# TensorE's order in the last chunk of an attention and expert kernel: the early tokens' transposes moved, the first products spread over the last routing

## The chip, the core and the metric

The kernel runs on one core of a Trainium2 chip. A core has five engines with queues of their own: TensorE (PE), which multiplies matrices, VectorE (DVE), ScalarE (ACT), GpSimd (POOL) and SyncE (SP), which issues most transfers. Each engine executes its queue in order. Engines wait for each other by semaphores. The metric is the device time of one execution in microseconds; the time before is the median of three runs, 338.18 us (337.67 to 339.53).

## The reference

Two stages. The first is a linear attention with decay, over 4 batches, 8 heads, 768 steps and 48 dimensions a head:

```
for t in range(S):
    cur = einsum('bhd,bhe->bhde', u * kt, vt)
    y[:, :, t] = einsum('bhd,bhde->bhe', rt, state + cur)
    state = wt[..., None] * state + einsum('bhd,bhe->bhde', kt, vt)
```

The second takes the 3072 rows of y (384 wide). A row with `x @ w_skip > 0` goes to the expert, of eight, with the largest `x @ w_gate`; its output is `x + gate * (relu(x @ w1[e]) @ w2[e])`, with the softmax's value as gate and w1 of 384x1024, w2 of 1024x384. Other rows are copied.

## The kernel before

**Chunks.** The sequence is cut into 24 chunks of 128 steps (6 per batch). A loop over s from -2 to 24 (L545) runs a software pipeline with everything in the order in which it is written: in turn s the keys of chunk s+2 are scaled (`prep_*`, DVE), the scores of chunk s+1 are made (`intra`, L292, PE) and masked (`mask`, L298, DVE), the bonus of the current step is made (`bonus_sums`, L307, PE; `bonus`, L311, DVE, which writes it to PSUM as the start of y), and y of chunk s is summed on top of it (`outputs`: L342 from the scores, L347 from the state). `evict` (L352, ACT) copies y, `rows_out` (L357, PE) turns it into rows with the logits beside them, and `store` (L365, L367, ACT; L368, SP) takes logits and rows out one turn later.

**Routing.** Chunks are routed in four groups of six. `router` is a generator: `drip` runs it on by one piece at a time, from places between the steps above, and `flush` emits what it left for PE or ACT in the list `held`. It makes the one-hot of each row's expert (`oh`, L398), each row's rank within its expert by small products on PE (`ranks`, L401 to L406, to the bank `pss`), one-hots of the ranks (`hot`, L436), the gates in three parts (`vals`, L423, L446, L449), and with them tables of row numbers and gates by expert and rank (`places`, L459 and L462).

**The early expert.** After three groups (`LATE` = 18 chunks) expert 0 has 128 tokens already. `early` gathers their rows (L488, POOL, to `xg0`); `early_tokens(0)` transposes them (L502, PE, in a PSUM buffer of the two that bear the tag `psT`, which `rows_out` and the keys' transposes share) and copies them to `xT0` (L503, ACT). `early_expert` is a generator too, of 24 first-layer products of 128x128 (L112 by `hidden`, in two groups of 12, each evicted twice by ACT, L521 and L523, and once by DVE, L510), and 24 second-layer products (L532). Each yields a price, 214 or 160.

**The last routing.** After the loop, from L623, the last group's router runs alone. Each turn there drips it, flushes, adds `STEP` to the account `due` and emits early products until their prices have used it up. Then come the indices (`idr`, L633, DVE), the gather of expert 0's second 128 tokens (L615, POOL, `xg1`), the early products that remain but for the last four, the transposes of the second tokens (`early_tokens(1)`, L502), and the four.

**Experts.** The experts follow in order (`expert`), with expert 0's second tokens first (L112 again, then L733 to L735); each uses weights in a high and a low part (split on ACT and DVE, L86 and L87), and its rows are gathered by POOL (L615) and scattered back (L677).

Of the kernel before, what the change touches and what calls it, by code (L numbers as in the profile page):

```python
# [32 lines left out]
Q_MAX = 1e12  # L33
LATE = 18
NHB = 11
STEP = 230
W_AT = 4
Q_MIN = 1e-30
RW = 1 + NP * CW + 3 * NP * P + 3
# [14 lines left out]
def rwkv_moe_kernel(ctx, tc, wrk, wrk0, vN, uP, wgs, wgp, w12, cst, out):  # L54
# [7 lines left out]
    n = len(seq)  # L62
# [47 lines left out]
    def hidden(ps, xT, fc, kc):  # L110
        o = kc * DF + fc * P
        return nc.tensor.matmul(ps, raws[0, 0][:, o:o + P], xT[:, kc], start=(kc == 0),  # L112
                                stop=(kc == KC - 1))
# [5 lines left out]
    with tc.tile_pool(name="att", bufs=2) as att, \  # L119
# [105 lines left out]
        def drip(k=1):  # L225
            for _ in range(k):
                while later and next(later[0], None) is None:
                    later.popleft()

        work, lgs, gens = {}, {}, {}  # L230
        pace = [1]
# [38 lines left out]
        def prep_check(i):  # L270
            wk = work[i]
            w3 = wk["w"][:, 1:1 + NP * CW].rearrange("p (a j) -> p a j", a=NP)[:, :, :P]
            junk = att.tile([P, NP, P], BF16, tag="junk", name=f"junk{i}", bufs=1)
            nc.scalar.activation(junk, w3, AF.Relu, bias=bias_lo, scale=-1.0,
                                 accum_out=viol[:, i:i + 1])
            nc.scalar.copy(q0all[:, i], wk["q"][:, :, 0])
# [200 lines left out]
        def early():  # L477

            ps = ps1.tile([P, 512], F32, tag="psT", name="psC", bufs=2)[0:1, 0:1]
            nc.tensor.matmul(ps, onesb[:, 0:1], ohs[:, 0, 0:1], start=True, stop=True)  # L480
            short = att.tile([1, 1], F32, tag="short", name="short", bufs=1)
            nc.vector.tensor_scalar(short, ps, -1.0, float(P), op0=ALU.mult, op1=ALU.add)
            yield 1
            nc.vector.scalar_tensor_tensor(ohs[0:1, 0, 0:1], short, 0.0, ohs[0:1, 0, 0:1],
                                           op0=ALU.max, op1=ALU.add)
            yield 1
            nc.vector.tensor_tensor(id0, tab[:, 0, 0, 0:1], tab[:, 0, 1, 0:1], op=ALU.add)
            nc.gpsimd.indirect_dma_start(  # L488
                out=xg[0], out_offset=None, in_=out[:LATE * P],
                in_offset=bass.IndirectOffsetOnAxis(ap=id0, axis=0),  # L490
                bounds_check=LATE * P - 1, oob_is_err=False)
            yield 1
            nc.vector.tensor_reduce(gate0, tab[:, 0, 2:NV, 0], axis=AX, op=ALU.add)
            for _ in range(6):
                yield 1
            early_tokens(0)
            yield 1

        def early_tokens(j):
            ps = ps1.tile([P, KC, P], F32, tag="psT", name=f"psX0{j}", bufs=2)  # L500
            for kc in range(KC):
                nc.tensor.transpose(ps[:, kc], xg[j][:, kc * P:(kc + 1) * P], ident)  # L502
            nc.scalar.copy(xT0[j], ps)  # L503
# [9 lines left out]
        def early_expert():  # L513
            for g in range(2):
                ps = ps1.tile([P, NP, P], F32, tag=f"psA{g}", name=f"psH0_{g}")
                for f in range(NP):
                    for kc in range(KC):
                        hidden(ps[:, f], xT0[0], NP * g + f, kc)
                        yield 214
                fs = slice(NP * g, NP * (g + 1))  # L520
                nc.scalar.activation(h0h[:, fs], ps, AF.Relu)  # L521
                hf = att.tile([P, NP, P], F32, tag="asb", name=f"hf{g}", bufs=4)
                nc.scalar.activation(hf, ps, AF.Relu)  # L523
                hfs.append((h0l[:, fs], hf, h0h[:, fs].bitcast(F32)))
            pso = ps1.tile([P, DM], F32, tag="psB", name="psO0")
            w2h, w2l = wsp[0, 2], wsp[0, 3]
            todo = [(h0h, fc, w) for fc in range(FC) for w in (w2h, w2l)]
            todo += [(h0l, fc, w2h) for fc in range(FC)]
            for i, (h, fc, w) in enumerate(todo):
                if i == len(todo) - FC:  # L530
                    early_low(FC)
                nc.tensor.matmul(pso, h[:, fc], w[:, fc * DM:(fc + 1) * DM],  # L532
                                 start=(i == 0), stop=(i == len(todo) - 1))
                yield 160
            nc.vector.scalar_tensor_tensor(fin0, pso, gate0, xg[0], op0=ALU.mult, op1=ALU.add)
# [6 lines left out]
        with tc.manual_schedule():  # L542
            setup()
            fill(FILL0)
            for s in range(-2, n + 1):  # L545
                on = lambda i: 0 <= i < n
                if s + 4 < n:
                    load_chunk(s + 4)
                if on(s + 3) and s + 3 >= 1:
                    load_v(s + 3)  # L550
                if s == -2:
                    nc.sync.dma_start(c_sb[:, C_IOTA:], cst[:, C_IOTA:])
                    nc.sync.dma_start(wgp_sb, wgp)
                if s == -1:
                    nc.sync.dma_start(wgs_sb, wgs)
                if on(s - 1):
                    store(s - 1)
                for i0, m in GROUPS:
                    if i0 + m == s:
                        pace[0] = 1 if i0 + m < LATE else 2  # L560
                        later.append(router(i0, m))
                        if i0 + m == LATE:
                            later.append(early())
                if on(s):
                    update(s)
                    carry(s)
                if on(s + 2):
                    prep_scan(s + 2)
                drip(pace[0])
                if on(s):  # L570
                    outputs(s)
                flush()
                if on(s + 2):
                    prep_keys(s + 2)
                    drip(pace[0])
                    prep_reads(s + 2)
                if on(s):
                    evict(s)
                if on(s + 1):
                    intra(s + 1)  # L580
                    drip(2 * pace[0])
                    mask(s + 1, 0)
                    mask(s + 1, 1)
                    drip(pace[0])
                    bonus_sums(s + 1)
                    bonus(s + 1)
                if on(s + 2):
                    prep_check(s + 2)
                if on(s):
                    rows_out(s)  # L590
                flush()
                if s == -2:
                    nc.vector.tensor_copy(trib, tri)
                    nc.gpsimd.tensor_copy(identb, ident)
                    nc.gpsimd.tensor_copy(iota, c_sb[:, C_IOTA:C_IOTA + 2 * P])
                k = s + 1 - W_AT
                for eq, k0 in (((0, 1), 0), ((0, 0), 3), ((1, 0), 8), ((1, 1), 16)):
                    if k == k0:
                        gens[eq] = load_weights(*eq)
                    if k0 <= k < k0 + 3:  # L600
                        next(gens[eq])
                if 1 <= k < 7:
                    split_slice(0, 5 + k, nc.gpsimd)
                if 9 <= k < 15:
                    split_slice(1, k - 9, nc.gpsimd)
# [15 lines left out]
        ids = keep.tile([P, 2, E], U32, name="ids")  # L621
        gates = keep.tile([P, 2, E], F32, name="gates")
        with tc.manual_schedule(engines={nc.tensor.engine, nc.scalar.engine, nc.vector.engine}):  # L623
            todo, due, done = early_expert(), 0, [0]
            while later:
                drip(pace[0])
                flush()
                due += STEP
                while due > 0:
                    due -= next(todo, 1 << 20)  # L630
                    done[0] += 1
            with nc.allow_low_precision(reason="whole numbers"):
                nc.vector.tensor_reduce(idr, pt[:, :, 0:2].rearrange("p j q e -> p j e q"),  # L633
                                        axis=AX, op=ALU.add)
            gather(1, None)
            early_low(1)
            nc.vector.tensor_reduce(gates, pt[:, :, 2:].rearrange("p j q e -> p j e q"),
                                    axis=AX, op=ALU.add)
            nc.vector.tensor_scalar(idf, gates, 0.0, BIG, op0=ALU.is_equal, op1=ALU.mult)
            nc.vector.tensor_tensor(ids, idf, idr, op=ALU.add)  # L640
            for k in range(done[0], 6 * FC - 4):
                next(todo)
            early_tokens(1)
            drain(todo)
# [269 lines left out]
```

## Time and profile before

| | |
|---|---|
| median of three runs | 338.18 us (337.67 to 339.53) |
| the profiled execution, its time | 338.03 us |
| its span, first to last instruction | 336.2 us |
| mean granted clock of PE | 0.951 of full speed |
| PE busy | 300.8 us (89%) |
| DVE, ACT, POOL busy | 253.4, 174.6, 85.9 us |
| read and written in HBM | 52.76 and 7.86 MB |

The span starts at 0; times in the rows below are microseconds from there, durations in nanoseconds are called so. A row of the timeline gives the start, the length, the engine and line, the operation, what it writes and reads, and how many instructions are merged in it; a bracket tells how long the engine stood idle ahead of it and what ended that. A product in full precision is two instructions of PE in the profile (x6 is three products). The granted clock is the share of full speed at which PE's clock ran in a stretch. In the span, chunks end near 180 us, the last routing near 187, and experts fill the rest.

### The profile page before, as it was taken

To read this page: it belongs to the slowest core of one execution; us is meant where nothing else is said; L and a number is where in the kernel's file an instruction comes from. 1 tells how busy PE (TensorE), PEld (TensorE's weight loads), DVE (VectorE), ACT (ScalarE), POOL (GpSimd) and SP (SyncE) were. 2 spreads that over 40 slices of the span, in tenths; PEclk is the share of its full clock that TensorE was granted. 3 is DMA by queue.
4 is the path that set the end of the run, shared out by engine and by line. 5 is a ranking of instruction groups with operands and counts; after the bars stand their busy time and mean duration, and the time that the engine had idled before them with its cause. 6 is when DMAs were issued, how large, how long until landed. Compare 5 with 4: busy or idle time off the path is not lost.

```text
span 336.2 us, 7539 instructions
## 1 busy us (share of the span) xinstructions
PE 300.8 (89%) x2845; PEld 279.7 (83%) x2845; DVE 253.4 (75%) x472; ACT 174.6 (52%) x479; POOL 85.9 (26%) x88
## 2 busy tenths in 40 slices
PE   7499998898979989599696999999999999999990
PEld 2388887897869878488585999999999999999990
DVE  5899999899998999999524357859494949585410
ACT  4357666586384864556612255838282828273300
POOL 7312124433233334211200177240202020111111
PEclk9789999799997999979969899999999999999996
DMA  8999999999999887783301149984736373630000
GB/s 234 247 228 216 252 249 263 242 244 210 187 283 254 179 186 162 149 221 111 110 2 47 25 128 329 391 289 144 259 112 261 106 257 126 256 153 23 7 27 12
DMA packets 23104, 60.40 MB, mean 180 GB/s; under 512 B 4103, under 2 KB 10667, under 8 KB 23057
## 3 DMA queue, kind: packets, MB, share of 16 engines
q1 hardware_dynamic: 20576, 53.69, 59.4%
q0 software_dynamic: 2048, 5.48, 4.9%
q10 hardware_dynamic: 432, 0.66, 0.6%
q8 instruction: 24, 0.39, 0.5%
q14 instruction: 24, 0.19, 0.2%
HBM read 52.76 MB, written 7.86 MB: 180 GB/s over the span
## 4 chain that ended last, share of the span: by engine, by line
PE 59%; DMA 19%; DVE 9%; issue 5%; POOL 4%; SPq 2%; ACT 0%; POOLq 0%; DVEq 0%
DMA vt<-wrk 10%; DMA wrk<-wrk 7%; PE psO L735 6%; PE psO L733 6%; PE psO L734 6%; PE psH L715 6%; PE psH L714 6%; PE psH L713 6%; PE psY L342 4%; PE psY L347 3%; PE psA L292 3%; PE psB L307 3%; PE psH L112 3%; POOL rk L262 2%; DVE asb L298 2%
## 5 line engine op out<-in xcount | busy, mean ns | idle before, releaser
L262 POOL TENSOR_TENSOR rk<-wrk 128x512 f32<-128x512 f32 x24 | 30.7, 1279 | 105.8 <-PE psA L292 31.8
L720 ACT ACTIVATE hh<-psH 128x256 fp32r<-128x256 f32 x60 | 23.0, 383 | 55.8 <-PE psH L715 52.5
L715 PE MATMUL psH<-xTh,w1l 128*128 128x256 f32 x168 | 47.5, 283 | 0.0
L714 PE MATMUL psH<-xTl,w1h 128*128 128x256 f32 x168 | 47.5, 283 | 0.0
L713 PE MATMUL psH<-xTh,w1h 128*128 128x256 f32 x168 | 47.5, 283 | 0.0
L677 POOL DMA_INDIRECT out<-fin,ids x16 | 16.8, 1049 | 101.6 <-DVE fin L740 94.7
L342 PE MATMUL psY<-asb,v 128*48 128x128 f32 x384 | 28.2, 294 | 14.2 <-DVE psY L311 14.1
L733 PE MATMUL psO<-w2h,hh 128*128 128x384 f32 x120 | 40.7, 339 | 0.0
L298 DVE TENSOR_TENSOR asb<-psA,c_sb 128x512 f32<-128x512 f32 x48 | 30.8, 683 | 12.8 <-PE psA L292 12.8
L735 PE MATMUL psO<-w2h,hl 128*128 128x384 f32 x120 | 40.1, 334 | 0.0
L734 PE MATMUL psO<-w2l,hh 128*128 128x384 f32 x120 | 40.1, 334 | 0.0
L242 DVE TENSOR_TENSOR_SCAN q<-wrk,smask 128x516 f32<-128x516 f32 x24 | 34.4, 1435 | 3.7 <-DMA wrk<-wrk 3.7
L342 PEld LDWEIGHTS psY<-asb,v 128*48 128x48 f32 x384 | 21.9, 132 | 16.2 <-DVE psY L311 15.7
L721 DVE SCALAR_TENSOR_TENSOR hl<-psH,hh 128x256 fp32r<-128x256 f32 x60 | 25.2, 420 | 12.2 <-ACT hh L720 11.8
L715 PEld LDWEIGHTS psH<-xTh,w1l 128*128 128x128 f32 x168 | 32.2, 192 | 0.0
L714 PEld LDWEIGHTS psH<-xTl,w1h 128*128 128x128 f32 x168 | 32.2, 192 | 0.0
L713 PEld LDWEIGHTS psH<-xTh,w1h 128*128 128x128 f32 x168 | 32.2, 191 | 0.0
L292 PE MATMUL psA<-rp,kq 64*128 64x128 f32 x384 | 29.6, 296 | 1.2 <-DVE rp L259 1.2
L740 DVE SCALAR_TENSOR_TENSOR fin<-psO,gates,xg 128x384 f32<-128x384 f32 x15 | 9.3, 618 | 28.3 <-PE psO L735 28.3
L292 PEld LDWEIGHTS psA<-rp,kq 64*128 64x128 f32 x384 | 25.0, 199 | 5.7 <-issue 3.9
L255 DVE TENSOR_TENSOR_SCAN rh<-wrk,dstart 128x516 f32<-128x516 f32 x24 | 29.3, 1223 | 0.0
L87 DVE TENSOR_TENSOR w2l<-r,w2h 128x512 fp32r<-128x512 f32 x42 | 27.8, 687 | 1.1 <-ACT w2h L86 0.2
(137 smaller groups left out, 658.3 us busy)
## 6 DMA issues: line engine op xcount, KB each, us to landing
r<-w SPq DMA_DIRECT2D x48, 512.0 KB, 5.6
wrk<-wrk SPq DMA_DIRECT2D x46, 288.9 KB, 5.9
v<-vN SPq DMA_DIRECT2D x24, 192.0 KB, 5.6
out<-x SPq DMA_DIRECT2D x24, 192.0 KB, 5.0
vt<-wrk SPq DMA_DIRECT2D x46, 96.0 KB, 5.7
wrk<-wrk SPq DMA_DIRECT2D x1, 258.5 KB, 3.9
wrk<-wrk ACTq DMA_DIRECT2D x1, 256.0 KB, 4.1
wrk<-wrk SPq DMA_DIRECT2D x1, 256.0 KB, 4.6
```

Of the source, the lines that this page charges most:

```text
L242: nc.vector.tensor_tensor_scan(q.rearrange("p a j -> p (a j)")[:, ::-1], t[:, 1:1 + n_][:, ::-1], smask_f[:, ::-1], 0.0, op0=ALU.mult, op1 ...
L255: nc.vector.tensor_tensor_scan(rh.rearrange("p a j -> p (a j)"), wk["w"][:, 0:NP * CW], dstart.rearrange("p a j -> p (a j)"), 0.0, op0=ALU ...
L262: mul = nc.gpsimd.tensor_tensor(rk.rearrange("p a j -> p (a j)"), wk["w"][:, R_OFF:K_OFF], wk["w"][:, K_OFF:V_OFF], op=ALU.mult)
L292: nc.tensor.matmul(wk["psa"][g][:, a], wk["kq"][rows, a], wk["rp"][rows, a], start=True, stop=True)
L298: nc.vector.tensor_tensor(s, wk["psa"][g], tri.rearrange("p (o j) -> p o j", o=1).to_broadcast([P, NP, P]), op=ALU.mult)
L342: nc.tensor.matmul(psy[64 * g:64 * g + D, a], v[:, 2 * a + g], wk["asb"][g][:, a], start=False, stop=(c == 0), skip_group_check=True)
L713: nc.tensor.matmul(ps, w1h[:, o:o + P], xTh[:, kc], start=(kc == 0), stop=False)
L714: nc.tensor.matmul(ps, w1h[:, o:o + P], xTl[:, kc], start=False, stop=False)
L715: nc.tensor.matmul(ps, w1l[:, o:o + P], xTh[:, kc], start=False, stop=(kc == KC - 1))
L733: nc.tensor.matmul(pso, h[j, fc][0], w2h[:, o], start=(fc == 0), stop=False)
L734: nc.tensor.matmul(pso, h[j, fc][0], w2l[:, o], start=False, stop=False)
L735: nc.tensor.matmul(pso, h[j, fc][1], w2h[:, o], start=False, stop=(fc == FC - 1))
```

## The change

Two edits in TensorE's order. `early_tokens(0)` was called by `early`, six pieces after its gather, and is now called in the turn of the last chunk, between `evict` and `rows_out`. And the account of the last routing starts at `HEAD * STEP` = 1284 instead of 0, gets 214 a turn instead of 230, and each turn drips the router by one piece instead of two (`pace` is 2 there).

```diff
-STEP = 230
+HEAD = 6
+STEP = 214
@@ early()
             nc.vector.tensor_reduce(gate0, tab[:, 0, 2:NV, 0], axis=AX, op=ALU.add)
-            for _ in range(6):
-                yield 1
-            early_tokens(0)
             yield 1
@@ the loop over s
                 if on(s + 2):
                     prep_check(s + 2)
+                if s == n - 1:
+                    early_tokens(0)
                 if on(s):
                     rows_out(s)
@@ the last routing
-            todo, due, done = early_expert(), 0, [0]
+            todo, due, done = early_expert(), HEAD * STEP, [0]
             while later:
-                drip(pace[0])
+                drip()
                 flush()
                 due += STEP
                 while due > 0:
                     due -= next(todo, 1 << 20)
                     done[0] += 1
```

Lines behind L36 have numbers one higher in the changed kernel, up to L493, and two lower from there to L586 (L502 becomes L500, L112 L113, L342 L343, L532 L530).

PE's queue from the state update of chunk 22 (psu) to the first scores of chunk 23 (psA_23), before. The psX at L502 is the early tokens' transpose, xg_65 their gathered rows:

```order
L320 MATMUL psu<-v_1959,kt_2223 48x48 x8
L502 MATMUL psX_2277<-c_sb,xg_65 128x128 x3
L342 MATMUL psY<-asb_22_2240,v_1959 48x128
L342 MATMUL psY<-asb_22_2242,v_1959 48x128 x2
L342 MATMUL psY<-asb_22_2240,v_1959 48x128 x2
L342 MATMUL psY<-asb_22_2242,v_1959 48x128 x2
L342 MATMUL psY<-asb_22_2240,v_1959 48x128
L347 MATMUL psY<-rp_2110,sblk_110 128x128 x4
```

Now y of chunk 22 follows the update directly; the three transposes are gone from here.

The same queue from the rows of chunk 22 (the first psX) to the start of the last ranks (trib), before, and then of the change. psH is the bank of the early first-layer products, xT_67 the early tokens' transpose:

```order
L357 MATMUL psX_2316<-wgp_sb,xT_2294 128x105 x4
L112 MATMUL psH_0_2366<-xT_67,r_00_816 128x128 x3
L342 MATMUL psY<-asb_23_2306,v_2063 48x128
L342 MATMUL psY<-asb_23_2308,v_2063 48x128 x2
L342 MATMUL psY<-asb_23_2306,v_2063 48x128 x2
L342 MATMUL psY<-asb_23_2308,v_2063 48x128 x2
L342 MATMUL psY<-asb_23_2306,v_2063 48x128
L347 MATMUL psY<-rp_2212,sblk_111 128x128 x4
L357 MATMUL psX_2340<-wgp_sb,xT_2338 128x105 x4
L401 LDWEIGHTS trib
```

```order
L358 MATMUL psX_2311<-wgp_sb,xT_2289 128x105 x4
L343 MATMUL psY<-asb_23_2301,v_2063 48x128
L343 MATMUL psY<-asb_23_2303,v_2063 48x128 x2
L343 MATMUL psY<-asb_23_2301,v_2063 48x128 x2
L343 MATMUL psY<-asb_23_2303,v_2063 48x128 x2
L343 MATMUL psY<-asb_23_2301,v_2063 48x128
L348 MATMUL psY<-rp_2212,sblk_111 128x128 x4
L500 MATMUL psX_2335<-c_sb,xg_65 128x128 x3
L358 MATMUL psX_2340<-wgp_sb,xT_2333 128x105 x4
L113 MATMUL psH_0_2364<-xT_67,r_00_816 128x128 x10
L402 LDWEIGHTS trib
```

The transposes stand between y and the rows of chunk 23; three early products have left the place ahead of its y, and ten stand between its rows and the ranks, where none stood.

From the last product of the ranks to the first of the places, before, and then of the change:

```order
L406 MATMUL pss<-oh_2373,onesb 128x8
L112 MATMUL psH_0_2366<-xT_67,r_00_816 128x128 x7
L459 LDWEIGHTS identb
L459 MATMUL pss<-tab,identb 128x40
L462 LDWEIGHTS hot_0_2396
```

```order
L407 MATMUL pss<-oh_2380,onesb 128x8
L113 MATMUL psH_0_2364<-xT_67,r_00_816 128x128 x2
L113 MATMUL psH_1_2397<-xT_67,r_00_816 128x128 x12
L460 LDWEIGHTS identb
L460 MATMUL pss<-tab,identb 128x40
```

Fourteen early products instead of seven stand here, and all 24 are now ahead of the places; the 14 that followed the places before are gone from there, so that the second-layer products (L532) follow directly. On ACT the evictions of the first group of twelve (L521 and L523) now precede the last routing's gate casts (L422, L423, L446), and on DVE their low part (L510) stands between the indices (L633) and the gates (L637). The queues of POOL and SP are the same.

## The prediction

> **What bounds the kernel now.** I read three views in this order: the engines' busy time by stretch, the rows in order of time around the places where TensorE (PE) has nothing to do, and busy time again on the grid on which the granted clock moves. The first asks whether a gap on PE can be made good later.
>
> ```profile
> span 336.2 us, 7539 instructions
> 200.00:250.00 50.00, 50.00 (x368) 50.00 (x367) 37.67 (x72) 30.00 (x67) 15.32 (x15) 1.00 0.70 248
> ```
>
> From 200 to 250 us (columns: length, busy time of PE, weight loads, DVE, ACT and POOL, then granted clock, DMA share, GB/s) PE works all the time at full clock. What follows the last routing is one queue on PE, so whatever brings the expert products forward brings the end forward. The question is when PE reaches them, and where it stands before. Columns of the next rows: start, length, engine, line, operation; in brackets the idle time ahead and what ended it.
>
> ```profile
> 158.33 1.04 PE L342 MATMUL psY<-asb,v 128*48 128x128 f32 x16
> 159.31 1.16 PE L347 MATMUL psY<-rp,sblk 128*128 128x128 f32 x8
> 161.07 1.16 PE L292 MATMUL psA<-rp,kq 64*128 64x128 f32 x16
> 164.13 0.69 DVE L311 TENSOR_TENSOR psY<-psB,vt 128x512 f32<-128x512 f32 x1
> 164.46 1.23 POOL L488 DMA_INDIRECT xg<-out,id  x1 [0.17 <-issue]
> 168.04 0.87 PE L502 MATMUL psX<-c_sb,xg 128*128 128x128 f32 x3 [3.34 <-DMA xg<-out,id]
> 168.84 1.95 PE L342 MATMUL psY<-asb,v 128*48 128x128 f32 x16
> 170.72 2.08 PE L347 MATMUL psY<-rp,sblk 128*128 128x128 f32 x8
> 172.72 1.57 PE L292 MATMUL psA<-rp,kq 64*128 64x128 f32 x16
> 175.53 0.69 DVE L311 TENSOR_TENSOR psY<-psB,vt 128x512 f32<-128x512 f32 x1
> 176.09 0.85 PE L112 MATMUL psH<-xT,r 128*128 128x128 f32 x6
> 176.88 1.08 PE L342 MATMUL psY<-asb,v 128*48 128x128 f32 x16
> 179.72 1.14 PE L357 MATMUL psX<-wgp_sb,xT 128*128 128x105 f32 x8 [0.68 <-ACT xT L352]
> ```
>
> The transposes of the early tokens (L502) stand ahead of chunk 22's y products (L342), and PE waits 3.34 us for the gather that feeds them. The y products needed only the bonus of DVE (L311), done at 164.13 + 0.69 = 164.82. After the gap they run slowly: 168.84 to 172.80 for y and state reads, where chunk 21 took 158.33 to 160.47. The clock says why. On a grid of 3.41 us, each stretch shows one clock:
>
> ```profile
> 57.59:61.00 3.41, 1.37 (x25) 1.06 (x20) 3.41 (x7) 2.84 (x10) 2.50 (x2) 1.00 1.07 291
> 61.00:64.41 3.41, 3.41 (x20) 3.08 (x21) 3.12 (x7) 1.35 (x3) 0.03 (x1) 0.50 1.03 203
> 78.07:81.48 3.41, 1.88 (x32) 1.66 (x32) 3.41 (x5) 2.19 (x8) 2.32 (x2) 1.00 1.03 201
> 81.48:84.89 3.41, 3.41 (x43) 2.98 (x40) 3.38 (x7) 1.59 (x6) 0.00 (x0) 1.00 1.03 227
> 163.40:166.81 3.41, 1.29 (x24) 1.06 (x22) 1.42 (x4) 2.23 (x8) 2.12 (x2) 1.00 0.27 78
> 166.81:170.23 3.42, 2.19 (x17) 1.88 (x19) 0.00 (x0) 0.48 (x1) 0.00 (x0) 0.50 0.10 37
> 180.47:183.88 3.41, 1.24 (x17) 1.08 (x16) 2.46 (x12) 1.12 (x5) 0.00 (x0) 1.00 0.16 58
> 183.88:187.29 3.41, 3.23 (x28) 3.08 (x27) 2.62 (x14) 0.21 (x1) 0.02 (x1) 0.50 0.00 0
> ```
>
> After a stretch with 1.24 to 1.37 us of PE work the clock is halved, after one with 1.88 it is not. Two gaps of this kernel cost that: the one at 164.7, and the routing's, in these rows:
>
> ```profile
> 182.77 0.21 DVE L398 TENSOR_TENSOR oh<-key,km 128x48 bf16<-128x48 f32 x1
> 183.03 0.18 PE L401 MATMUL pss<-oh,trib 128*128 128x48 bf16 x1 [2.17 <-DVE oh L398]
> 183.21 2.75 PE L112 MATMUL psH<-xT,r 128*128 128x128 f32 x14
> 185.71 0.41 DVE L452 TENSOR_TENSOR sg<-oh,vals 128x240 bf16<-128x240 bf16 x1
> 186.17 0.36 PE L462 MATMUL pss<-sg,hot 128*128 128x40 bf16 x6 [0.18 <-DVE sg L452]
> 186.60 3.69 PE L112 MATMUL psH<-xT,r 128*128 128x128 f32 x28
> 186.80 0.19 DVE L633 TENSOR_REDUCE idr<-pss 128x16 uint32<-128x32 f32 x1 [0.69 <-PE pss L462]
> 187.27 1.00 POOL L615 DMA_INDIRECT xg<-out,idr  x1 [21.59 <-DVE gates L637]
> 193.65 0.49 PE L502 MATMUL psX<-c_sb,xg 128*128 128x128 f32 x3
> 195.05 5.52 PE L112 MATMUL psH<-xT,r 128*128 128x128 f32 x48
> ```
>
> PE waits 2.17 us for the one-hot of experts (L398), works at half clock, and goes without a gap from 186.60 into the products of the second early token tile, at 195.05. That last start is the mark that I carry through the change.
>
> **The change, first part: transposes moved behind y of chunk 23.** No instruction is added or removed; on DVE, ACT and POOL nothing else moves in this part but the copy after the transposes, and no queue of SP or POOL is passed. Chunk 22's y starts at about 164.88 instead of 168.84. At full clock its y and state reads take 2.14 us as for chunk 21 (160.47 − 158.33), so they end at 167.0; its masks, keys, v and state were ready by then, because their row for the bonus, the last of them, is. The scores of chunk 23 take 1.16 as in the row at 161.07, to 168.2. From the end of the scores to the end of the bonus before: 172.72 + 1.57 = 174.29 to 175.53 + 0.69 = 176.22, that is 1.93 of DVE work. So the bonus ends at 170.1 and y of chunk 23 starts at 170.15. Three early products filled PE before this start (0.85 at 176.09); they are gone from here, and PE now rests some 0.2 us at most. From y to the logits' rows it took 179.72 − 176.88 = 2.84, of which 0.68 was a wait for ACT's copy of y. The transposes cost 0.49 (row at 193.65, full clock) and fit in that wait: they are free, and would cost 0.49 if ACT's copy were earlier. Their tokens land at 168.0, some 4 us before they are needed at 172.3. The rows of chunk 23 start at 173.0 instead of 179.72: **6.7 us earlier**. From the other side: 4.0 (start of y) + 1.8 (half clock in y and reads) + 0.4 (scores) + 0.6 (three products) = 6.8.
>
> **Second part: the 24 first products.** One costs 5.52/24 = 0.23 us at full clock; the row of 14 instructions at half clock (7 products in 2.75) bounds it at 0.39. Counting from the rows' start, with 179.72 set to 173.0:
> - ten products now follow the rows: 1.1 + 2.3 = 3.4 after the start. The ranks ran at 3.31 before. Their wait of 2.17 is filled, at a cost of 0.1.
> - 14 instead of seven products stand between ranks and places: 0.2 + 3.2 more, so PE is free for the places at 6.8. The place values (sg) were ready at 186.12, 6.4 after the start. ACT has 1.2 us of evictions more ahead of the gate's casts:
>
> ```profile
> 187.64 0.60 ACT L521 ACTIVATE h0h<-psH 128x512 fp32r<-128x512 f32 x1 [2.17 <-PE psH L112]
> 188.13 0.59 ACT L523 ACTIVATE hf<-psH 128x512 f32<-128x512 f32 x1
> ```
>
>  Their group of twelve products ends some 0.5 after the ranks, so they end near 5.2 after the start. DVE's six one-hots take until then anyway: I take 0.2 for the casts, and the places wait for PE, not for sg. Without that cover the casts would cost up to 1.2.
> - places, 0.43 as before (186.60 − 186.17), then the indices 0.2 later (186.80 − 186.60): PE goes on at 180.3, the indices start at 180.5 and the gather of the second tile at 180.5 + 0.47 = 180.97.
>
> **What is late next.** The 14 products that ran while that gather was under way are gone from behind the places. PE now has only 20 products of the second layer there. Their length is in the chain of waits, and the gather's, from issue to landing, is the last number in the rows of DMA issues; the row of three numbers is for all 15 gathers of line 615:
>
> ```profile
> 190.28 3.53 PE psO L532 x20
> ```
>
> ```profile
> xg<-out,id POOLq DMA_INDIRECT x1, 3.4
> xg<-out,idr POOLq DMA_INDIRECT x1, 4.0
> DMA to landing us min/median/max: 3.0/6.5/8.2
> ```
>
> So PE would come to the transposes at 180.3 + 3.5 = 183.8. The same gather took 4.0, so I take that: landing at 185.0, and PE waits **1.2 us, new**. Behind it in PE's queue stand four second-layer products and all experts. With 3.0, the fastest, the wait is 0.2. From these transposes to the next tile's products it was 195.05 − 193.65 = 1.40, so those start at 186.4.
>
> **Sum.** 195.05 − 186.4 = 8.65 us earlier: 6.7 from the first part, some 3.1 from a routing that no longer waits and runs at full clock, less 1.2 for the new wait. I set it against the profiled execution, 338.03 us (span 336.2 and 1.8 around it): 338.03 − 8.65 = 329.4. The median of the runs shown, 338.18, lies 0.15 above, within what runs differ.
>
> One rule bears on the new wait. In the Trainium skill, "TensorE: Matmul & The Clock Gate", Part 1, the clock halves after an idle window of some 3.4 us; by that alone the 2.17 us at 183.03 would not have halved it, and the wait of 1.2 never could. The trace agrees on the 3.41 but not on the idleness: 1.24 us of work did not save that stretch. Part 4 of that page says that transposes do not count as busy in the same way; no run here shows it.
>
> **Rivals.**
> - *The new wait halves the clock.* If PE's transposes did not count, a stretch of 3.41 with the wait of 1.2 and 0.5 of transposes would have 1.7 us of work, between 1.37 (halved) and 1.88 (not). The price is the next 3.41 us at half speed: 1.7 us, 331.1. Against it: with the transposes it has 2.2, and a stretch that the wait straddles has more. The page's Part 4 is what speaks for it.
> - *The second tile's gather is later.* The row at 187.27 names the gates (L637) as releaser, and 0.69 of DVE work (the low part of the first group) now stands ahead of them: 0.9 more if true; and the slowest landing of such a gather was 8.2, 4.2 more. That gives 330.3 to 333.6. Against it: the gather reads indices, not gates, and nothing else moves on DMA then.
> - *The gain is given back behind 195 us*, by a transfer that doesn't come forward with PE: 336.5 to 338. Against it: the gathers of the other experts and the next weights are released by PE's and DVE's own progress, and PE shows 50.00 of 50.00 there.
> - *Slower than before.* The rows of chunk 23, and with them the whole routing, now stand behind the first gather. If it lands after 172.3, every microsecond costs one; the kernel is slower from a landing at 172.3 + 8.6 = 180.9, which is 16.4 after its issue at 164.46. It took 3.4; the slowest of its kind took 8.2. At a landing of 182 the time would be 339.
> - *The change does not do what it says*: excluded by the order of the instructions, which shows each move.
>
> **How the numbers follow.** My forecast, 328.4 (gather in 3.0) to 330.4, has 0.71. The halved clock has 0.12, the late gather 0.08, the gain given back 0.06, slower 0.02; 0.01 is left below. The range runs from 328.4 to 331.5, which holds the first two and the cheaper half of the third. A measurement of this kernel tells about 0.5%, 1.7 us, from no change. Faster by more than that needs less than 336.5: 0.94; within it 0.04; slower 0.02.
>
> **What would show it.** Right: no PE gap near 165 to 168 and a full clock through both former half-clock stretches; the rows of chunk 23 at 173.0; the transposes between y and rows with no wait; ranks and places without a PE wait above 0.2; a wait of 0.2 to 1.2 at the second tile's transposes; its products at 186.4; and from there the same lengths as before. Wrong: a half clock after 184, a gather of the second tile that lands more than 4 us after its issue, or a new gap among the experts.

## The result, and the profile after

| | before | after |
|---|---|---|
| median of four runs | 338.07 us (337.67 to 339.53) | 328.90 us (328.49 to 329.58) |
| ratio, with its 95% interval | | 0.9723 (0.9697 to 0.9750) |
| the profiled execution: time, span | 338.03, 336.2 us | 328.79, 327.0 us |
| mean granted clock of PE | 0.951 | 0.970 |
| PE busy | 300.8 us (89%) | 296.9 us (91%) |

The kernel is 9.2 us faster; the forecast was 329.4. Below are the same places in the timeline of the changed kernel (start, length, engine, line, operation, and in brackets the idle time ahead and what ended it). Its chunk stage ran 0.43 us later, ahead of anything that was changed: the first row, chunk 22's state update, starts at 164.56, and at 164.13 before (over all traces here at 162.97 to 166.65). So starts are compared from that update on.

```profile
164.56 0.56 PE L321 MATMUL psu<-v,kt 128*48 128x48 f32 x16
165.31 1.08 PE L343 MATMUL psY<-asb,v 128*48 128x128 f32 x16 [0.18 <-DVE psY L312]
166.32 1.16 PE L348 MATMUL psY<-rp,sblk 128*128 128x128 f32 x8
167.41 1.16 PE L293 MATMUL psA<-rp,kq 64*128 64x128 f32 x16
170.55 1.08 PE L343 MATMUL psY<-asb,v 128*48 128x128 f32 x16
172.55 0.49 PE L500 MATMUL psX<-c_sb,xg 128*128 128x128 f32 x3
173.39 1.14 PE L358 MATMUL psX<-wgp_sb,xT 128*128 128x105 f32 x8 [0.35 <-ACT xT L353]
174.37 2.42 PE L113 MATMUL psH<-xT,r 128*128 128x128 f32 x20
176.70 0.18 PE L402 MATMUL pss<-oh,trib 128*128 128x48 bf16 x1
176.88 3.37 PE L113 MATMUL psH<-xT,r 128*128 128x128 f32 x28
179.57 0.41 DVE L453 TENSOR_TENSOR sg<-oh,vals 128x240 bf16<-128x240 bf16 x1
180.08 0.18 PE L460 MATMUL pss<-tab,identb 128*128 128x40 bf16 x1
180.63 0.19 DVE L633 TENSOR_REDUCE idr<-pss 128x16 uint32<-128x32 f32 x1 [0.65 <-PE pss L463]
181.10 1.20 POOL L615 DMA_INDIRECT xg<-out,idr  x1 [14.98 <-DVE idr L633]
184.65 0.52 PE L500 MATMUL psX<-c_sb,xg 128*128 128x128 f32 x3 [0.45 <-DMA xg<-out,idr]
185.98 5.62 PE L113 MATMUL psH<-xT,r 128*128 128x128 f32 x48
```

Read it from above. The wait of 3.34 for the first gather is gone: y (L343) follows the update at once, and y and reads take 1.08 and 1.16 where they took 1.95 and 2.08. The transposes (L500) stand before the rows (L358), and PE then waits 0.35 for ACT's copy where it waited 0.68. The ranks (L402) have no wait. The places (L460) start at 180.08, 0.10 after DVE's place values are ready (179.57 + 0.41 = 179.98): PE and DVE arrive together. The one new wait is the 0.45 at 184.65. The same stretches on the clock's grid (length, then busy time of PE, weight loads, DVE, ACT, POOL, then granted clock, DMA share, GB/s):

```profile
164.93:168.35 3.42, 3.24 (x50) 2.81 (x44) 0.32 (x1) 2.56 (x8) 1.19 (x1) 1.00 0.38 118
175.17:178.59 3.42, 3.42 (x37) 3.33 (x36) 3.11 (x18) 1.23 (x4) 0.00 (x0) 1.00 0.16 58
182.00:185.41 3.41, 2.96 (x19) 2.67 (x18) 0.56 (x1) 0.20 (x1) 1.99 (x3) 1.00 0.28 75
200.00:250.00 50.00, 50.00 (x357) 50.00 (x356) 36.76 (x69) 28.19 (x62) 9.58 (x10) 1.00 0.67 240
```

None of the first three, which hold the former gap at the gather, the ranks and the new wait, has less than 2.96 us of work, and the clock is 1.00 in all. Among the experts PE is busy 50.00 of 50.00, as before: nothing is given back there. From the second tile's products to the end of the span it takes 327.0 − 185.98 = 141.0, before 336.2 − 195.05 = 141.2. From the update to those products it takes 21.42, before 30.92: **9.50 less**. With the 0.43 lost ahead and the 0.13 won behind (unrounded) that is the span's 9.2.

### The profile page after: what moved, and what is told of

It reads as the page before. It is cut to its first block, busy times and chain, and to the rows that moved or that the text cites. A ratio compares the mean times of both kernels' runs of the same rounds, so it can differ in the third digit from the quotient of the medians.

```text
span 327.0 us, 7539 instructions
## 1 busy us (share of the span) xinstructions
PE 296.9 (91%) x2845; PEld 276.2 (84%) x2845; DVE 253.4 (77%) x472; ACT 174.5 (53%) x479; POOL 87.9 (27%) x88
## 4 chain that ended last, share of the span: by engine, by line
PE 64%; DMA 16%; DVE 10%; issue 5%; POOL 2%; SPq 1%; ACTq 0%; POOLq 0%; ACT 0%; DVEq 0%
DMA vt<-wrk 9%; PE psO L734 6%; PE psO L733 6%; PE psO L735 6%; PE psH L715 6%; PE psH L714 6%; PE psH L713 6%; DMA wrk<-wrk 5%; PE psY L343 5%; PE psY L348 4%; PE psA L293 4%; PE psH L113 3%; PE psB L308 3%; DVE asb L299 3%; DVE psY L312 2%
## 5 line engine op out<-in xcount | busy, mean ns | idle before, releaser
L263 POOL TENSOR_TENSOR rk<-wrk 128x512 f32<-128x512 f32 x24 | 31.6, 1318 | 104.7 <-PE psA L293 34.7
L343 PE MATMUL psY<-asb,v 128*48 128x128 f32 x384 | 27.3, 288 | 14.8 <-DVE psY L312 14.7
L243 DVE TENSOR_TENSOR_SCAN q<-wrk,smask 128x516 f32<-128x516 f32 x24 | 33.5, 1395 | 4.1 <-POOL wrk L198 2.2
L343 PEld LDWEIGHTS psY<-asb,v 128*48 128x48 f32 x384 | 21.3, 129 | 16.7 <-DVE psY L312 16.6
```

What stands on the lines that cost most here:

```text
L243: nc.vector.tensor_tensor_scan(q.rearrange("p a j -> p (a j)")[:, ::-1], t[:, 1:1 + n_][:, ::-1], smask_f[:, ::-1], 0.0, op0=ALU.mult, op1 ...
L263: mul = nc.gpsimd.tensor_tensor(rk.rearrange("p a j -> p (a j)"), wk["w"][:, R_OFF:K_OFF], wk["w"][:, K_OFF:V_OFF], op=ALU.mult)
L343: nc.tensor.matmul(psy[64 * g:64 * g + D, a], v[:, 2 * a + g], wk["asb"][g][:, a], start=False, stop=(c == 0), skip_group_check=True)
```

## The experiments

Theory T is the prediction's: the end follows one queue on PE; the first part brings the rows forward by removing a blocked transpose and a halved clock, the second fills the routing's waits. Unless a text on record says otherwise, every kernel below computes the whole reference. "Landmarks" are starts counted from chunk 22's state update: the rows of chunk 23, the ranks, and the second tile's products. Before they are 15.59, 18.90, 30.92; after 8.83, 12.14, 21.42.

The runs came in three groups, and the kernel before had a median of 349.24 us in the first (x1 to x4), 338.20 in the second (x5 to x8) and 338.93 in the third (x1b to x4b, the kernels of the first group once more). The landmarks are comparable in all; times are compared by ratios within a group.

### One part alone: x1, x1b and x2, x2b

x1 is the kernel before with the transposes moved; routing as before.

```diff
@@ early()
-            for _ in range(6):
-                yield 1
-            early_tokens(0)
             yield 1
@@ the loop over s
+                if s == n - 1:
+                    early_tokens(0)
                 if on(s):
                     rows_out(s)
```

> The first part alone: the early tokens' transposes stand between y and rows of chunk 23; the last routing runs as before (two pieces a turn, STEP 230, the account from 0). On PE three products then stand between the rows and the ranks, seven between ranks and places, 14 behind the places. My theory (stall, half clock and filled wait are the first part's, the routing's wait the second's): rows of chunk 23 start as in the changed kernel, 6.7 us earlier than before, and the routing keeps 1.5 us of its wait at the ranks; about 331.3 us, or 332 if that wait still halves the clock. Rival A (the stall is all of the gain, the products' places do nothing): 329. Rival B (only the stall's own 3.3 us count, not the clock): 334.7.

> The first part alone once more, since in its first runs the experts' stretch was slower in all kernels (their weights came late) and the times moved by some 5 us. My theory, now from the first traces: the second tile's products start 2.3 us later behind chunk 22's state update than in the changed kernel and 7.2 earlier than before; 330.9 us where the kernel before takes 338.1. Rival (the products' places do nothing): 329.

x2 has the second part alone: `HEAD`, `STEP` = 214 and one piece a turn, with the transposes where they were.

```diff
-STEP = 230
+HEAD = 6
+STEP = 214
@@ the last routing
-            todo, due, done = early_expert(), 0, [0]
+            todo, due, done = early_expert(), HEAD * STEP, [0]
             while later:
-                drip(pace[0])
+                drip()
```

> The second part alone: the transposes stay ahead of y of chunk 22, the routing's account starts at HEAD turns with 214 a turn and one piece a turn. On PE ten products then stand ahead of y of chunk 23, where three stood, since their tokens are there early; none stands between the rows and the ranks. My theory (the stall stays; ten products delay y of chunk 23 by 1.6 us; the wait at the ranks stays at 2.2 us and halves the clock for the 14 products behind it): no gain, 337 to 338.5. Rival (the parts add up): 9.2 less 6.7, so 335.6.

> The second part alone once more, for the same reason. My theory: the second tile's products start 0.5 us later behind chunk 22's update than before, so no gain, 338.6 us. Rival (the parts add up, as the first ratio of 0.994 would have it): 335.6 to 336.

Ratios to before: x1 0.9834 (0.9808 to 0.9861), x1b 0.9802 (0.9755 to 0.9849); x2 0.9936 (0.9899 to 0.9973), x2b 1.0001 (0.9965 to 1.0037). Landmarks: x1b 8.82, 12.13, 23.71 (x1 8.83, 12.15, 23.73); x2b 17.31, 20.62, 31.32 (x2 17.52, 20.83, 31.44). The timeline of x1b:

```profile
173.79 1.14 PE L357 MATMUL psX<-wgp_sb,xT 128*128 128x105 f32 x8 [0.35 <-ACT xT L352]
177.10 0.18 PE L401 MATMUL pss<-oh,trib 128*128 128x48 bf16 x1 [1.48 <-DVE oh L398]
180.23 0.31 PE L462 MATMUL pss<-sg,hot 128*128 128x40 bf16 x6 [1.12 <-DVE sg L452]
180.56 3.37 PE L112 MATMUL psH<-xT,r 128*128 128x128 f32 x28
```

The first part alone brings the rows as far forward as both do, at full clock. At the products it gains 30.92 − 23.71 = 7.21. Behind the rows PE waits 1.48 at the ranks and 1.12 at the places, because its 14 last products stand behind both (180.56), where they cover the second gather. 1.48 + 1.12 − 0.45 (the new wait, absent here) = 2.15 of the 2.29 us by which x1b's products start later than the changed kernel's. The rivals fall: no loss without the second part, a clock halved by the ranks' wait, and the one that counts only the stall's own 3.3, since the rows come 6.77 earlier. And of x2b:

```profile
176.61 2.42 PE L113 MATMUL psH<-xT,r 128*128 128x128 f32 x20
178.96 1.08 PE L343 MATMUL psY<-asb,v 128*48 128x128 f32 x16
185.11 0.20 PE L402 MATMUL pss<-oh,trib 128*128 128x48 bf16 x1 [2.17 <-DVE oh L399]
185.33 4.62 PE L113 MATMUL psH<-xT,r 128*128 128x128 f32 x28
```

Where the transposes are early, the ten products have their input early too, and the scheduler (the tool that fixes the order of the queues when the program is built; in the code the products stand behind the loop) places them ahead of y of chunk 23 (176.61) instead of behind its rows. There they push the rows back by 17.31 − 15.59 = 1.72, and the 2.17 at the ranks stays and halves the clock, as the 4.62 of 14 products shows (3.37 at full clock). The ratio of x2 alone, 0.9936, would fit the rival that adds the parts (335.6 of 338.1 is 0.9926). But in the trace of x2 too the second tile's products start later than before, at 31.44, so what its times won does not lie in the stretch that was changed, and x2b's ratio is 1.0001. So the second part alone is worth nothing, and some 2.3 us behind the first. The parts are not two independent gains; the rival that adds them falls.

### The halved clock alone: x3, x3b

x3 is the kernel before with 14 products of zeros, whose result nobody reads, ahead of the waiting transposes: the wait remains, the idleness goes.

```diff
@@ early()
+            fill(14)
             early_tokens(0)
```

> The kernel before, with 14 products of zeros (128x512 in bf16, results unused) put ahead of the early tokens' transposes, so that PE is busy while it waits for the gather and nothing comes earlier. My theory (2.5 us of the first part are the halved clock after the stall): transposes, y, reads and scores of chunks 22 and 23 at full clock, rows of chunk 23 2.5 us earlier, 335.6 us. Rival (the wait alone counts): no change, 338.1.

> The kernel before with the stall filled by unused products once more, for the same reason. My theory: the second tile's products start 3.0 us earlier than before, 335.1 us. Rival (the clock is not worth anything at the end, as the first ratio of 0.997 would have it): 337 to 338.1.

Ratios: x3 0.9967 (0.9933 to 1.0000), which decides nothing; x3b 0.9934 (0.9896 to 0.9972). The rows of chunk 23 come 2.5 us earlier in both (13.05 and 13.08): that much of the first part's 6.77 is the clock. The other 4.2 are the wait with the transposes' own 0.45 in it (y of chunk 22 starts 4.36 after the update in x3, 0.75 in the changed kernel: 3.6) and the three products ahead of y of chunk 23 (0.6). But the products of the second tile start at 27.95 in x3 and 30.30 in x3b, from the same program. Both waited the same at the ranks; first x3, then x3b, each with the 14 first products that follow the places:

```profile
181.86 0.18 PE L401 MATMUL pss<-oh,trib 128*128 128x48 bf16 x1 [2.18 <-DVE oh L398]
185.33 3.37 PE L112 MATMUL psH<-xT,r 128*128 128x128 f32 x28
```

```profile
181.69 0.18 PE L401 MATMUL pss<-oh,trib 128*128 128x48 bf16 x1 [2.17 <-DVE oh L398]
185.24 5.61 PE L112 MATMUL psH<-xT,r 128*128 128x128 f32 x28
```

In x3b these ran at half clock for most of their length. The windows on each run's own grid, x3's first, say why:

```profile
176.69:180.10 3.41, 2.32 (x18) 1.96 (x17) 0.16 (x1) 0.96 (x3) 0.00 (x0) 1.00 0.13 46
180.10:183.51 3.41, 1.65 (x20) 1.65 (x20) 3.10 (x17) 0.75 (x4) 0.00 (x0) 1.00 0.16 58
183.51:186.93 3.42, 2.29 (x32) 2.19 (x31) 2.02 (x12) 1.08 (x3) 0.94 (x1) 1.00 0.03 5
```

```profile
179.67:183.08 3.41, 1.39 (x18) 1.39 (x18) 3.00 (x15) 1.00 (x5) 0.00 (x0) 1.00 0.16 58
183.08:186.50 3.42, 2.70 (x26) 2.55 (x25) 2.27 (x13) 0.23 (x2) 0.58 (x1) 0.51 0.02 5
```

In x3 an edge of the grid (180.10) splits the wait, its stretch keeps 1.65 us of work, and the next has full clock. In x3b nearly the whole wait falls into one stretch, 1.39 is left, and the next is halved. Where the grid lies differs from run to run.

### Where the transposes stand: x4, x4b, x5

x4 is the changed kernel with `early_tokens(0)` behind `rows_out(s)` of the last chunk; x5 has it one chunk earlier, behind the rows of chunk 22.

```diff
-                if s == n - 1:
-                    early_tokens(0)
                 if on(s):
                     rows_out(s)
+                if s == n - 1:
+                    early_tokens(0)
```

> The changed kernel with the early tokens' transposes one place later, behind the rows of chunk 23 instead of ahead of them. My theory (ahead of the rows they fill the wait for ACT's copy of y and are free; behind them they and their copy delay the ten products, and so the ranks, by 1.1 us): 330.0 us. Rival (PE has slack there, the place does not matter): 328.9.

> The changed kernel with the early tokens' transposes behind the rows of chunk 23 once more, for the same reason. My theory: 1.0 us later than the changed kernel, 329.9 us. Rival (the place does not matter or is better, as the first ratio of 0.967 would have it): 327 to 328.9.

```diff
-                if s == n - 1:
-                    early_tokens(0)
                 if on(s):
                     rows_out(s)
+                if s == n - 2:
+                    early_tokens(0)
```

> The changed kernel with the early tokens' transposes one place earlier, behind the rows of chunk 22 and ahead of y of chunk 23; the ten early products then stand between y and the rows of chunk 23. My theory (the chain from the rows over the routing to the second gather sets the time, so what delays the rows costs): rows 1.8 us later than in the changed kernel, and the wait at the ranks is empty again; 330.8 us, or 332.3 if that wait halves the clock. Rival (PE's work bounds the stretch; products in place of idle time are a gain wherever they stand): 328.5.

Ratios: x4 0.9674 (0.9607 to 0.9741), but its four runs lie between 333.04 and 341.8 us, too wide to set against the changed kernel; x4b 0.9756 (0.9718 to 0.9794); x5 0.9821 (0.9782 to 0.9859). Landmarks: x4 8.83, 13.20, 22.46; x4b 8.82, 13.20, 22.58; x5 10.46, 13.67, 22.84. In x4b:

```profile
172.56 1.14 PE L358 MATMUL psX<-wgp_sb,xT 128*128 128x105 f32 x8 [0.68 <-ACT xT L353]
174.60 2.50 PE L113 MATMUL psH<-xT,r 128*128 128x128 f32 x20 [0.57 <-ACT xT L501]
```

The rows are as early as in the changed kernel, with the wait of 0.68 before them again: the transposes are free inside it, as the prediction had it. Behind the rows they cost their own 0.49 and a wait of 0.57 for ACT's copy, together the 1.06 by which the ranks are later. The second tile's products follow by 1.04 and 1.16. In x5, as in x2, the ten products slip ahead of chunk 23's rows, which start 1.63 later, and the 2.17 at the ranks is back; here it falls across an edge, and the clock stays full (1.95 and 2.71 us of work in the two stretches). The products start 1.42 later. That is the fastest of x5's four runs, 330.12 us; the others took 331.94 to 333.14, where a halved clock was expected to give 332.3, and whether it was halved in them no trace shows.

### How the 24 products are spread: x6, x7, x8

x6 and x8 change how much of the early expert stands behind the second tile's transposes, twelve and two second-layer products in place of four. x7 is the changed kernel with two pieces of the router a turn, as before, and so eight products before the ranks, seven between ranks and places, nine behind.

```diff
-            for k in range(done[0], 6 * FC - 4):
+            for k in range(done[0], 6 * FC - 12):
```

> The changed kernel with 12 of the early tokens' products left behind the transposes of the second tile instead of four, so that PE comes to these transposes 1.4 us earlier and waits about 1.9 us for the gather. My theory (the wait has no price of its own but the work pushed behind it; a stretch of the clock's grid keeps 1.5 us or less of work at worst): 330.3 us at full clock. Rival of the halved clock: half clock for 3.4 us behind the wait, 332.0.

```diff
-                drip()
+                drip(pace[0])
```

> The changed kernel with two pieces of the router a turn, as before: eight products stand between rows and ranks, seven between ranks and places, nine behind the places. My theory (the places wait for DVE's values, so the products moved behind them leave PE idle ahead of the places and only cover the gather's wait of 0.45): 330.2 us, 1.3 more than the changed kernel. Rival (the account's head start does it all): 328.9.

```diff
-            for k in range(done[0], 6 * FC - 4):
+            for k in range(done[0], 6 * FC - 2):
```

> The changed kernel with two of the early tokens' products behind the second tile's transposes instead of four. My theory (two more products, 0.35 us, fit into the gather's wait of 0.45, until ACT's copy of the transposes is late instead): 328.7 us, 0.2 less, too little to be told by times, but seen as a wait of 0.1 at the transposes. Rival (the wait moves with the work): the same wait of 0.45, 329.0.

Ratios: x6 0.9785 (0.9728 to 0.9842), x7 0.9753 (0.9713 to 0.9794), x8 0.9726 (0.9689 to 0.9763). The second tile's products start at 22.80, 22.71 and 21.33. One row of each shows the wait that decides; x6, x7, x8:

```profile
185.51 0.52 PE L500 MATMUL psX<-c_sb,xg 128*128 128x128 f32 x3 [1.82 <-DMA xg<-out,idr]
```

```profile
182.03 0.31 PE L463 MATMUL pss<-sg,hot 128*128 128x40 bf16 x6 [1.23 <-DVE sg L453]
```

```profile
184.31 0.52 PE L500 MATMUL psX<-c_sb,xg 128*128 128x128 f32 x3 [0.24 <-DMA xg<-out,idr]
```

x6 lengthens the new wait by 1.37, and the products start 1.38 later: a wait there costs its own length, and no halved clock. x7 shows what single turns are for: with too few products before and between, PE waits 1.23 for the place values (and 0.37 at the ranks). x8 shortens the wait by 0.21 and brings the products 0.09 forward; its time cannot be told from the changed kernel's. No version that beats the change was found. For x6's wait the stretch on the grid is this:

```profile
183.28:186.70 3.42, 1.60 (x11) 1.31 (x10) 0.18 (x1) 0.48 (x1) 2.00 (x2) 1.00 0.38 102
186.70:190.10 3.40, 3.40 (x29) 3.12 (x28) 0.67 (x2) 0.16 (x1) 2.57 (x3) 1.00 0.55 145
```

1.60 us of work, of which 0.52 are transposes, and full clock behind it. This is the rival "the new wait halves the clock" at its strongest: the prediction's 1.7 us of work left the transposes out, x6 has 1.60 with them, and the halving still did not come.

## Why the prediction was right

| step of the prediction, from the state update | predicted | measured |
|---|---|---|
| rows of chunk 23 | 8.87 (173.0) | 8.83 |
| gather of the second tile issued | 16.84 (180.97) | 16.54 |
| its landing after the issue | 4.0 (3.0 at the least) | 3.4 |
| PE free for the second tile's transposes | 19.67 (183.8) | 19.64 |
| new wait there | 1.2 | 0.45 |
| from the transposes to the products | 1.40 | 1.33 |
| second tile's products | 22.27 (186.4) | 21.42 |
| gain at that point | 8.65 | 9.50 |

- **First part.** 6.7 was predicted and 6.76 came. Its pieces are shown apart: x3b's 2.5 for the halved clock is made up of the prediction's 1.8 for y and reads and 0.4 for the scores, and 0.35 for the transposes themselves (0.45 from their start to y's in x3b, 0.80 before), which the prediction had within its 4.0 for the start of y; x4b shows that the transposes are free ahead of the rows and cost 1.06 behind them.
- **Second part.** The ten products filled the ranks' wait: the ranks started 3.31 after the rows, 3.4 were predicted. The places started 6.69 after them (predicted 6.8), with DVE's values 0.10 ahead. x1b shows the part to be worth 2.29 at the products; the prediction had 8.65 − 6.7 = 1.95 for the routing less the new wait, and 0.44 of the routing's gain came with the first part already (7.21 less the rows' 6.77), since in x1b no halved clock follows the ranks' wait. That it would be worth nothing alone was not in the prediction: x2b's order, ten products ahead of y, was not among the rivals, and had no part in the forecast.
- **Mis-sized: the new wait.** The step "the same gather took 4.0, so I take that" was 0.6 too long, and the gather was issued 0.3 earlier. That PE was free at 19.64, as predicted to 0.03, is luck: it came to the second layer 0.29 earlier (180.44 − 164.56 = 15.88, where 180.3 is 16.17), and the 20 products took 3.76 instead of 3.5. In the rows of DMA issues of the changed kernel, the last number is the time from issue to landing:

```profile
xg<-out,idr POOLq DMA_INDIRECT x1, 3.4
xg<-out,id POOLq DMA_INDIRECT x1, 4.6
```

 The 4.0 was the exception: in the other nine traces that show it, this gather took 3.3 to 3.6. So the term was sized from one landing; the range down to 328.4, from the bound of 3.0, took the difference in.
- **Rivals.** The gates do not release the second gather: its row at 181.10 names the indices (idr), and the prediction's doubt about the row before is settled. No clock is halved at the new wait, at 0.45 or, in x6, at 1.82. Nothing is given back among the experts. The first gather, which took 3.4 before, now took 4.6; it landed some 3 us before the transposes needed it (164.89 + 4.6 = 169.5 against 172.55), so the slower case was not near. In the Trainium skill, "TensorE: Matmul & The Clock Gate", Part 4, transposes do not count as busy in the same way; x6's stretch speaks against that here: without them it would have had between 1.08 us of work (1.60 − 0.52) and 1.33 (their rows overlap the next product's by 0.25), and no other stretch seen with so little kept the clock. It is one run, and the profile does not say whether these transposes ran in the transpose mode that the page speaks of.

## What to carry to other kernels

In an engine's queue that works in order, an instruction put early that waits for a transfer costs the wait of all that stands behind it; put it where the engine would stand still anyway, and behind work that doesn't need it. Work that fills waits has to be where the waits are, and its place depends on when its own inputs are ready: moving the inputs and spreading the work are one edit, not two (0.9802 and 1.0001 alone, 0.9723 together). Price a wait on TensorE by the work that is left in its stretch of the clock's grid, and not by its length, and count with both outcomes where a stretch may keep about 1.6 us.

## What the runs showed of the hardware that was not expected

- **The same wait halves the clock or does not, by chance.** A wait of 2.17 at the ranks did so in the kernel before, x2, x2b and x3b, and not in x3 (2.18) and x5, though x3 and x3b are one program. Of the stretches looked at that ran at full clock, those with up to 1.53 us of work were always followed by half clock, those with 1.86 and more never; between 1.59 and 1.76 both were seen. It cost x3b 2.35 us at the second tile's products. The four runs of the changed kernel stand in the order of their mean granted clock (328.49 us at 0.974, 328.79 at 0.970, 329.01 at 0.965, 329.58 at 0.962), which fits such chances but does not show them. In the Trainium skill, "TensorE: Matmul & The Clock Gate", Part 1, it takes an idle window of some 3.4 us; here 2.02 us of idleness in one stretch were enough (x3b's, 3.41 − 1.39).
- **The way back asks for more work.** Stretches at half clock with up to 2.78 us of work were followed by half clock again, those with 2.88 and more by full clock. So the wait for the first gather halved two stretches of the kernel before, not one. The first, from 166.81, had 2.19 us of work, and this is the second:

```profile
170.23:173.64 3.41, 3.41 (x22) 2.83 (x20) 0.00 (x0) 0.58 (x1) 0.00 (x0) 0.50 0.03 5
```

 The prediction's price for a halved clock at the new wait, one stretch and 1.7 us, holds only if that stretch is nearly full of work.
- **Expert work was slower in the first group, and why stays open.** It took longer there: from the second tile's products to the end of the span x1 took 151.8 us, x1b 141.0. The texts on record for the third group put this down to late weights. The trace of x1 doesn't bear that out: the median landing of its weights was 5.2 us, 5.3 in x1b, and it shows ACT idle ahead of evictions (L719) with no releaser on the core:

```profile
199.66 0.39 ACT L719 ACTIVATE hh<-psH 128x256 fp32r<-128x256 f32 x1 [3.40 <-remote]
206.71 0.38 ACT L719 ACTIVATE hh<-psH 128x256 fp32r<-128x256 f32 x1 [6.16 <-remote]
```

 Such waits come to 9.6 us in x1 and 9.5 in x3, but to 1.5 in x2 and 0.6 in x4, whose stretch to the end is 147.1 and 145.8 us, so they are not the whole of it. No other trace here has one. The kernel before was slower in that group too.
- **The first gather landed later where PE went on.** It carries 192 KB in every kernel. It took 3.4 to 3.5 us in the three traces in which PE waits for it (before, x2b, x3b), and 4.2 to 4.7 in the seven in which the transposes stand later. It cost nothing here, since the transposes needed it later still. What makes the difference no run shows.
